# Clearing six experts' unused rows after the routing instead of before it

## The chip, the cores and the metric

One core of a Trainium2 chip runs the whole network in one launch. Its engines work side by side, each on its own list of instructions in order: TensorE (PE; PEld is its weight load), VectorE (DVE), ScalarE (ACT), GpSimd (POOL) and SyncE (SP). SP computes nothing here; it issues nearly all transfers, which 16 DMA engines carry out, and it takes its list in order too: an issue that waits holds up all behind it. The metric is the device time of one execution in microseconds (us); lower is better.

## The reference, cut to what matters

```python
for t in range(S):                                   # attention, 32 heads, 768 steps
    y[:, :, t] = einsum(r_t, state)
    Sa = einsum(state, a_t)
    state = state * w_t - Sa b_t + v_t k_t
...
expert_idx = argmax(x @ w_gate)                      # 3072 tokens, 8 experts
for i in range(N):                                   # each expert's rows, in order of arrival
    if counts[e] < capacity:
        disp[e, counts[e]] = x[i]; counts[e] += 1
h = maximum(einsum(disp, w1), 0); y = einsum(h, w2)  # all rows of disp, unused ones are zero
out[i] = gate_w[i] * y[expert_idx[i], pos[i]]
...
g = elu(x @ w_in); return g @ w_out                  # feed-forward, d_ff 2048
```

`disp` starts as zeros: rows that no token takes are zero. The capacity is 768 rows an expert.

## The kernel before

The kernel has three stages: the attention, the eight experts, and the feed-forward layer on tokens sorted by expert.

**The attention** cuts the sequence into 24 units of 64 steps (two halves of the batch, 12 chunks). Its order is written out by hand: the string `ORDER` and then `slot(k)` name steps by a letter and a unit, and each name issues the next part of that step. Every engine executes its own part of that list in order. `e`, `v`, `d` load inputs (L230, L234, L238); `p`, `a` scale them (VectorE L243 to L255, ScalarE L264); `c` makes score matrices and stores them to memory (L277, L291); `l` loads them back in the layout of the solve (L330); `i` is the triangular solve on GpSimd (L351, L353) for a group of two or four units; `o` stores its result (L359), and `t` loads that (L374 to L385); `f`, `g` complete the inverse; `r`, `u`, `w`, `s`, `q`, `y`, `x` make the unit's output and the next state; `b`, `j` find each token's expert and row. `D` scatters the unit's tokens to their rows of `disp` in memory with an indirect transfer of GpSimd.

`disp` has eight regions of `ES` = 3,584 rows of 329 numbers, one an expert; an expert's tokens start at row `ES * e + SL`, with `SL` = 448. `Z` followed by an expert's number is `zero_d` (L619): a store of zeros over the expert's 448 rows from that start, from a small cleared piece of memory on the chip, in 752-byte pieces. All eight `Z` stand ahead of the first scatter `D`: `Z7` early, `Z2`, `Z4`, `Z3`, `Z0`, `Z6`, `Z5`, `Z1` among the preparation of units 8 to 12.

**The experts** run as blocks b = 0 to 7 of `run`. A block loads its 448 rows (L1084) one block ahead, at step 0 of the block before. It has 8 steps f. In each, TensorE makes the hidden layer (L968) and, three steps later, the second product (L1031 to L1041); ScalarE and VectorE make the two parts of the hidden layer (L1097, L1098). At f = 0 and 4 SP fetches half an expert's weights (L801, L803), and ScalarE and GpSimd split earlier ones into two parts (L775, L780). After its last product a block stores its rows to `xt`, sorted by expert, at columns whose start stands in a register (L1206 to L1208).

`more(b, f)`, called at the end of each step, does two other things. `counts()` (`ct`) makes the experts' counts from the routing, their running sums (`cs`, `bi`, L1340, L1341), the number of rounds, and loads registers of SP with the sums at b = 1, f = 2 (L1355). `rest` converts the feed-forward layer's weights from 64-bit numbers: loads (L822, L825), eight operations of VectorE for each piece (L858 to L870), stores (L830, L834); it begins at b = 0, f = 5. Its first call there issues the loads of the first three pieces, and its operations stand in VectorE's list before that step's later work.

**The feed-forward stage** loads sorted columns from `xt`, multiplies, and scatters the result.

Of the kernel before, what the change touches and what calls it, by code (L numbers as in the profile page):

```python
# [8 lines left out]
F32 = mybir.dt.float32  # L9
F32R = mybir.dt.float32r  # L10
I32 = mybir.dt.int32
U32 = mybir.dt.uint32
AF = mybir.ActivationFunctionType
ALU = mybir.AluOpType
# [8 lines left out]
SL = 448  # L23
ES = 8 * SL
RW = 329
# [7 lines left out]
KR = 5  # L33
ORDER = """
se1 sa0 se0 se0 v1 sc0 e0.0 sv se1 e0.1 sd p0 sw p0 e1.0 sw a0 p0 v0 p1 sa1 sx a0 p1 lw sz st1 e2.0 c0.0 a1
p2 p2 a1 c0.0 e1.1 sr1 Z7 c0.1 p1 e3.0 c0.1 k0.0 k0.1 c0.1 c1.0 e2.1 a2 a2 c1.0 p3 c1.1 k1.1 k1.0 c1.1 k1.0 e4.0 d1 k1.1
c1.1 e3.1 m0.0 l0 m0.1 k0.1 p2 p3 a3 l1 a3 p4 p4 p3 m1.1 c2.1 e5.0 k2.1 c2.0 c2.1 m1.0 r0 c2.0 k2.0 k0.0 a4 m2.1 a4 p5
st0 k2.0 k3.1 sc1 c3.0 c2.1 c3.1 ss1 k3.0 e4.1 m2.0 p4 r0 r1 c4.0 i0 e6.0 k3.0 n0 k3.1 m3.0 k4.1 p5 n1 o0 c3.1 p6
c3.0 e5.1 a5 a5 c3.1 m3.1 k2.1 r1 e7.0 l2 p5 k4.1 c4.1 k4.0 m4.1 e6.1 c4.0 c5.1 k5.1 l3 p6 k5.0 c5.0 c4.1 p7 c4.1 p6 a6
m5.0 a6 v2 v3 p7 c5.0 t1 m4.0 t0 c6.1 m6.1 c5.1 k4.0 f1 k6.1 c5.1 k6.0 k6.1 m5.1 sr0 a7 i1 c6.0 f1 f0 a7 o1 e7.1 e8.0 f1 f0  # L40
k5.0 p7 c6.1 f0 f1 f1 p8 c6.0 d0 e9.0 f0 k5.1 c7.1 f0 f1 f1 c6.1 c7.0 f0 f0 e8.1 c7.1 g1 c7.0 g0 p8 m7.0 a8 ss0 p8 m7.1
g0 k7.1 l5 l4 g1 k7.0 k7.1 g0 k8.0 g0 c7.1 l6 p9 e9.1 g1 a8 u0 m6.0 p9 k6.0 k8.1 u0 g1 l7 c8.0 k7.0 m8.0 c8.1 n2 t2 e10
w0 a9 p9 f2 n3 k8.1 a9 q0.0 w0 q0.1 q0.1 w0 i2 u1 u1 f2 q0.0 c8.0 f2 p10 k9.1 c9.1 f2 c8.1 c9.0 m8.1 k8.0 Z2 c8.1 f2 w0
Z4 p10 t3 f2 s0 k9.1 p10 c9.1 c9.0 w1 w1 k9.0 y0 f2 i2 k9.0 g2 s0 w1 e11 s0 c9.1 f3 k10.1 Z3 r2 a10 w1 a10 f3 k10.1 m9.0
f3 y0 m9.1 k10.0 p11 Z0 r2 c10.0 q1.0 q1.0 c10.1 x0 f3 p11 h2 q1.1 s1 f3 g2 a11 k10.0 m10.1 i2 f3 c10.0 g2 q1.1 c10.1 h2
e12 v4 p11 f3 s1 c10.1 x0 y1 y1 d2 g3 p12 a11 s1 k11.1 c11.0 x1 g3 r3 Z6 c11.0 g2 g3 p12 k11.1 h3 x1 m11.0 a12 Z5 p12 x0 r3
u2 a12 c11.1 c12.0 u2 g3 w2 d3 c11.1 w2 k11.0 w2 x1 k12.1 h3 q2.0 q2.1 Z1 b0 w2 c11.1 c12.1 u3 c12.1 m10.0 m11.1 s2 j0
o2 u3 w3 k11.0 q2.1 q3.1 c12.0 e13 z2 q2.0 s2 w3 y2 s2 l11 j0 l10 y2 t4 m12.0 m12.1 r4 v5 l9 g4 d4 w3 k12.1 r4 p13 D0
h4 x2 l8 g4 c12.1 k12.0 D1 h4 t5 q3.0 p13 w3 g4 g4 g4 s3 u4 x2 a13 l12 s3 z3 q3.0 u4 w4 w4 a13 q3.1 p13 i3 w4 g5 h5 y3
d5 x2 w4 y3 s3 s4 i3 k12.0 e14 t6 s4 s4 h5 v6  # L50
# [635 lines left out]
def consts(p):  # L686

    c = {}
    c["ident"] = p.tile([128, 128], F32, name="ident")
    c["mask"] = p.tile([128, 64], F32, name="mask")  # L690
    for nm in ("ones", "tri"):
        c[nm] = p.tile([128, 128], BF, name=nm)
    c["desc"] = p.tile([128, 8], F32, name="desc")
    c["ebase"] = p.tile([128, 8], F32, name="ebase")
    c["lg"] = p.tile([128, 24, 9], F32, name="LG")
    c["oh"] = p.tile([128, 2, 8, 12], BF, name="OH")
    c["slot"] = p.tile([128, 24], I32, name="SLOT")
    c["acc"] = p.tile([128, 2, 8], BF, name="ACC")
    c["cap"] = p.tile([128, 2], I32, name="CAP")
    return c  # L700
# [42 lines left out]
class Ring:  # L743
# [8 lines left out]
    def next(s, split):  # L752
        k = s.turn[split]
        s.turn[split] += 1
        return s.tile((1, 4, 6, 8)[k % 4], F32R) if split else s.tile((0, 3)[k % 2], F32)
# [39 lines left out]
def expert(nc, ring, w1, w2, e, paired=True):  # L795
    def load(g, R):
        q = R.rearrange("p (f x) -> p f x", x=704)
        c = slice(512 * g, 512 * g + 512)
        for k, (o, r, m) in enumerate(((0, 0, 128), (0, 128, 128), (0, 256, 64), (64, 256, 64))):
            k = min(k, 2)  # L800
            nc.sync.dma_start(out=q[o:o + m, :, 128 * k:128 * k + 128],  # L801
                              in_=w1[e, r:r + m, c].rearrange("p (f x) -> p f x", x=128))
        nc.sync.dma_start(out=q[:, :, 384:704], in_=w2[e, c, :].rearrange("(f p) d -> p f d", p=128))  # L803
    return Weights(nc, ring, load, 8, paired)
# [73 lines left out]
def ahead(W):  # L878

    W.fetch(0)  # L880
    yield
    yield from W.split(0)
    W.fetch(1)


def ffn(tc, nc, cst, disp, xt, w1, w2, w32, out, ring, W0, cv):
# [3 lines left out]
    ap = ctx.enter_context(tc.tile_pool(name="fa", bufs=2))  # L890
# [289 lines left out]
            B.finish([p[1:] for p in lag])  # L1180


    dv = disp.rearrange("(e r i p) d -> e r p i d", e=8, i=4, p=112)

    W2 = Weights(nc, ring, lambda g, R: nc.sync.dma_start(out=R, in_=w32[g]), 16)

# [2 lines left out]
    def experts(r, dyn=False, more=None):  # L1189
# [43 lines left out]
        def extra(b, f):  # L1233
            if b >= 8:
                next(final, None)
                return
            if b == 0 and f > 1:
                next(first, None)
            i, ph = divmod(8 * b + f, 4)

            late = {(14, 0): 16, (14, 2): 17, (15, 2): 18}.get((i, ph)) if i > 13 else i + 2 if ph == 0 else None
            if late:
                gen[0] = split(late)
                fetch(late + 1)
            go(gen[0], 1 if i < 14 else 2)
            if more:
                more(b, f)
# [76 lines left out]
    over = {}  # L1324

    def counts():

        cw, cf = cst["cap"], ap.tile([128, 4], F32, name="cf", bufs=1)
        nc.vector.tensor_copy(cf[:, 0:2], cw)
        nc.vector.tensor_scalar(cf[:, 2:3], cf[:, 0:1], 0.0, 4294967296.0, op0=ALU.is_lt, op1=ALU.mult)  # L1330
        nc.vector.scalar_tensor_tensor(out=cf[:, 3:4], in0=cf[:, 1:2], scalar=4294967296.0, in1=cf[:, 2:3], op0=ALU.mult, op1=ALU.add)
        nc.vector.tensor_tensor(cf[:, 3:4], cf[:, 3:4], cf[:, 0:1], op=ALU.add)
        over["cap"] = cf[:, 3:4]
        p = ps.tile([128, 512], F32, tag="ph", name="pc")
        nc.tensor.matmul(p[:, 0:8], cst["ones"], cst["acc"][:, 0], start=True, stop=True)
        yield
        cnt = over["cnt"] = ap.tile([128, 8], F32, name="cnt", bufs=1)
        nc.vector.tensor_copy(cnt, p[:, 0:8])
        cs, bi = ap.tile([128, 8], F32, name="cs", bufs=1), ap.tile([128, 8], I32, name="bi", bufs=1)
        nc.vector.tensor_tensor_scan(out=cs, data0=over["one"], data1=cnt, initial=0.0, op0=ALU.mult, op1=ALU.add)  # L1340
        nc.vector.tensor_copy(bi, cs)  # L1341
        yield
        rn = ap.tile([128, 4], F32, name="rn", bufs=1)
        ri = ap.tile([128, 1], I32, name="ri", bufs=1)
        rg = ap.tile([128, 8], F32, name="rg", bufs=1)
        nc.vector.tensor_reduce(rn[:, 0:1], cnt, axis=AX.X, op=ALU.max)
        nc.vector.tensor_scalar(rn[:, 1:2], rn[:, 0:1], float(SL // 8), None, op0=ALU.add)
        nc.vector.tensor_scalar(rn[:, 2:3], over["cap"], float(SL), None, op0=ALU.min)
        nc.vector.tensor_tensor(rn[:, 2:3], rn[:, 0:1], rn[:, 2:3], op=ALU.is_gt)
        yield  # L1350
        nc.vector.tensor_scalar(rg, cst["ebase"], 1.0 / 8, rn[:, 1:2], op0=ALU.mult, op1=ALU.is_lt)
        nc.vector.tensor_reduce(rn[:, 3:4], rg, axis=AX.X, op=ALU.add)
        nc.vector.tensor_scalar(ri, rn[:, 3:4], rn[:, 2:3], 1.0, op0=ALU.mult, op1=ALU.add)
        yield
        _, over["base"] = nc.values_load_multi_w_load_instructions(bi[0:1, 0:7], (mybir.EngineType.SP,), min_val=0, max_val=NTOK)  # L1355
        yield
        over["n"] = nc.values_load(ri[0:1, 0:1], min_val=1, max_val=8)
# [47 lines left out]
    rest = cv.pieces(scratch, 28)  # L1405

    def more(b, f):
        if b == 0 and 0 < f < 5 or b == 1 and f in (2, 7):
            next(ct, None)
        if b or f > 4:  # L1410
            for _ in range(1 + f % 2):
                next(rest, None)
    one = over["one"] = ap.tile([128, 8], F32, name="one", bufs=1)
    nc.gpsimd.memset(one, 1.0)
    start = over["start"] = ap.tile([128, 6], F32, name="begin", bufs=1)
# [4 lines left out]
    cst["turn"] = ap.tile([128, 1], F32, name="turn", bufs=1)  # L1420
    nc.gpsimd.memset(cst["turn"], 0.0)
    ct = counts()
    experts(0, more=more)
    for _ in rest:
        pass
# [26 lines left out]
def network(tc, nc, e_in, v_tok, d_in, wg, cap, w1, w2, w_in, w_out, out):  # L1452
    with tc.tile_pool(name="cst", bufs=1) as p, tc.tile_pool(name="dsp", bufs=1, space=DRAM) as dp, tc.manual_schedule():
        cst = consts(p)
        disp = dp.tile([8 * ES, RW], F32, name="disp")
        xt = dp.tile([D + 1, XC], F32, name="xt")
        ring = Ring(p)
        w32 = dp.tile([4, 128, 2816], F32, name="w32")
        W0, cv = expert(nc, ring, w1, w2, 0), Convert(nc, w_in, w_out, w32)
        attention(tc, nc, e_in, v_tok, d_in, wg, disp, xt, cst, ring, ahead(W0), W0, cv, cap)  # L1460
        ffn(tc, nc, cst, disp, xt, w1, w2, w32, out, ring, W0, cv)
# [26 lines left out]
```

## Time and profile before

| | us |
|---|---|
| median of 3 runs | 1,066.04 (1,063.58 to 1,072.04) |
| the profiled execution | 1,064.33 |
| its span, first to last instruction | 1,062.6 |
| around the span | 1.7 |
| TensorE busy in the span | 965.8 (91%) |
| VectorE | 727.8 (68%) |
| GpSimd | 606.5 (57%) |
| ScalarE | 516.9 (49%) |
| mean granted TensorE clock, of 1 | 0.941 |

Times in the rows below count from the start of the span. A row of an engine in order of time gives its start, its length, the engine, the line, the operation, what it writes and reads, how many are merged (x), and in brackets how long the engine stood idle just before it and who released it. The share of busy time is an average over stages with different limits, so the stages are read one by one.

### The profile page before, as it was taken

What the parts mean: (1) busy time and instruction counts of PE and PEld (TensorE: products, weight loads), DVE (VectorE), ACT (ScalarE), POOL (GpSimd) and SP (SyncE); (2) the same over time, 40 slices, a digit from 0 to 9 for tenths busy, and PEclk for the clock granted to TensorE, in tenths of its full rate; (3) what the DMA queues carried; (4) which work ended last, traced back from release to release, by engine and by line L of the source; (5) the groups of instructions that cost most, each with busy time, mean ns of one, the idle gap of its engine ahead of it and who ended that gap; (6) DMA issues with size and microseconds to landing.
All of it is one profiled execution on the core that took longest, in us unless ns stands there. A gap on an engine that the chain in (4) does not pass through costs nothing.

```text
span 1062.6 us, 25351 instructions
## 1 busy us (share of the span) xinstructions
PE 965.8 (91%) x9995; PEld 871.9 (82%) x9995; DVE 727.8 (68%) x1287; ACT 516.9 (49%) x1011; POOL 606.5 (57%) x926
## 2 busy tenths in 40 slices
PE   5869978899899999888999999989999999999993
PEld 4758877798788889677889888869989989989983
DVE  8856756788674677549798963656766767776751
ACT  4646544556463334244535545454555455554551
POOL 4757839899898813456677876733323333323332
PEclk9866988899899889999999999989999999999997
DMA  6768675667654864576877765400101010100000
GB/s 165 163 179 197 168 137 105 151 131 141 139 110 103 192 164 103 155 203 168 230 218 209 221 193 188 161 23 3 48 1 32 19 26 25 26 25 1 26 1 28
DMA packets 180984, 121.67 MB, mean 115 GB/s; under 512 B 105792, under 2 KB 166872, under 8 KB 179224
## 3 DMA queue, kind: packets, MB, share of 16 engines
q1 hardware_dynamic: 176788, 102.89, 39.6%
q0 software_dynamic: 3168, 11.14, 3.0%
q10 hardware_dynamic: 900, 5.93, 2.2%
q8 instruction: 81, 1.33, 0.6%
q14 instruction: 47, 0.39, 0.1%
HBM read 86.87 MB, written 33.05 MB: 113 GB/s over the span
## 4 chain that ended last, share of the span: by engine, by line
PE 28%; issue 10%; POOL 6%; DVE 6%; DMA 4%; ACT 2%; SPq 1%; POOLq 0%; DVEq 0%; ACTq 0%
PE ph L968 14%; PE po L992 4%; PE po L994 4%; PE po L993 4%; POOL ring L780 3%; POOL L L1112 2%; DMA ring<-in_w_dram 2%; DVE L L1098 1%; ACT ring L775 1%; SPq L801 1%; DMA S<-in_w_in_dram 1%; DMA w<-E 1%; POOL out_dram L1282 1%; DVE E L859 1%; DVE M L867 1%
## 5 line engine op out<-in xcount | busy, mean ns | idle before, releaser
L780 POOL TENSOR_TENSOR ring<-ring,ring 128x64 fp32r<-128x64 f32 (+2 forms) x320 | 195.7, 647 | 90.0 <-ACT ring L775 87.7
L1112 POOL TENSOR_TENSOR L<-E,H 128x512 fp32r<-128x512 f32 x66 | 87.6, 1327 | 185.8 <-ACT H L1111 148.2
L968 PE MATMUL ph<-XH,ring 128*128 128x512 f32 (+1 forms) x640 | 172.9, 392 | 4.4 <-DVE L L1098 3.9
L968 PEld LDWEIGHTS ph<-XH,ring 128*128 128x128 f32 x640 | 117.4, 193 | 19.6 <-DVE L L1098 4.5
L1105 ACT ACTIVATE E<-N 128x512 f32<-128x512 f32 x96 | 60.7, 633 | 143.7 <-DVE N L1104 88.0
L992 PE MATMUL po<-ring,H 128*128 128x320 f32 x384 | 119.6, 311 | 5.5 <-ACT Y L1044 5.3
L353 POOL TENSOR_TENSOR X<-X,ring 128x60 f32<-128x60 f32 (+19 forms) x170 | 114.9, 676 | 13.3
L994 PE MATMUL po<-ring,L 128*128 128x320 f32 x384 | 119.6, 311 | 1.5 <-POOL L L1112 1.5
L993 PE MATMUL po<-ring,H 128*128 128x320 f32 x384 | 119.4, 311 | 0.0
L1104 DVE TENSOR_SCALAR N<-ph 128x512 f32<-128x512 f32 x96 | 65.9, 686 | 47.4 <-PE ph L968 47.0
L968 PE MATMUL ph<-XL,ring 128*128 128x512 f32 (+1 forms) x320 | 97.6, 386 | 0.0
L968 PE MATMUL ph<-XS,ring 128*128 128x512 f32 (+1 forms) x320 | 97.5, 386 | 0.0
L351 POOL TENSOR_TENSOR ring<-X,ring 128x60 f32<-128x60 f32 (+19 forms) x108 | 74.2, 687 | 39.0 <-DMA ring<-dab 18.2
L992 PEld LDWEIGHTS po<-ring,H 128*128 128x128 f32 x384 | 72.6, 189 | 10.5 <-ACT Y L1044 5.7
L993 PEld LDWEIGHTS po<-ring,H 128*128 128x128 f32 x384 | 72.7, 189 | 4.1
L994 PEld LDWEIGHTS po<-ring,L 128*128 128x128 f32 x384 | 72.9, 190 | 2.0 <-POOL L L1112 2.0
L1109 DVE SCALAR_TENSOR_TENSOR M<-E,M 128x512 f32<-128x512 f32 x96 | 70.7, 736 | 5.5 <-ACT M L1106 5.5
L775 ACT CAST ring<-ring 128x704 fp32r<-128x704 f32 x80 | 61.4, 779 | 21.3 <-issue 8.2
L1110 DVE SCALAR_TENSOR_TENSOR E<-ph,M 128x512 f32<-128x512 f32 x96 | 66.4, 691 | 7.8
L968 PEld LDWEIGHTS ph<-XL,ring 128*128 128x128 f32 x320 | 61.1, 191 | 10.8
L968 PEld LDWEIGHTS ph<-XS,ring 128*128 128x128 f32 x320 | 60.8, 190 | 10.8
L1111 ACT CAST H<-E 128x512 fp32r<-128x512 f32 x96 | 59.2, 617 | 15.1 <-DVE E L1110 12.0
(238 smaller groups left out, 2164.2 us busy)
## 6 DMA issues: line engine op xcount, KB each, us to landing
ring<-in_w_dram SPq DMA_DIRECT2D x16, 640.0 KB
ring<-in_w_dram SPq DMA_DIRECT2D x32, 256.0 KB
RVU<-in_d_in_dram SPq DMA_DIRECT2D x48, 160.0 KB
dab<-AB SPq DMA_DIRECT2D x24, 256.0 KB
ring<-in_e_in_dram ACTq DMA_DIRECT2D x18, 321.6 KB
ring<-w SPq DMA_DIRECT2D x4, 1408.0 KB
disp<-ring SPq DMA_DIRECT2D x8, 575.8 KB
ring<-in_w_dram SPq DMA_DIRECT2D x32, 128.0 KB
```

The source lines that it names most:

```text
L351: nc.gpsimd.tensor_tensor(tv, X[:, 0:n, s:s + 1].to_broadcast([128, n, m]), N[:, s:s + 1, s + 1:e].to_broadcast([128, n, m]), op=ALU.mult)
L353: nc.gpsimd.tensor_tensor(X[:, 0:n, s + 1:e], X[:, 0:n, s + 1:e], tv, op=ALU.subtract)
L775: s.nc.scalar.copy(B[:, 0:704], r)
L780: s.nc.gpsimd.tensor_tensor(B[:, to], r[:, q], B[:, q].bitcast(F32), op=ALU.subtract)
L968: nc.tensor.matmul(p, l, r[:, 0:s.T], start=i == 0, stop=i == len(seq) - 1)
L992: nc.tensor.matmul(o, H[:, c], hb, start=f == 0, stop=False)
L993: nc.tensor.matmul(o, H[:, c], lb, start=False, stop=False)
L994: nc.tensor.matmul(o, L[:, c], hb, start=False, stop=f == s.W.nf - 1)
L1104: nc.vector.tensor_scalar(N, p, 0.0, None, op0=ALU.min)
L1109: nc.vector.scalar_tensor_tensor(out=M, in0=E, scalar=1.0, in1=M, op0=ALU.add, op1=ALU.mult)
L1110: nc.vector.scalar_tensor_tensor(out=E, in0=p, scalar=0.0, in1=M, op0=ALU.max, op1=ALU.add)
L1112: eng.tensor_tensor(L, E, H.bitcast(F32), op=ALU.subtract)
```

## The change

Six of the eight `Z` leave the order of the attention; `Z0` stands where `Z7` stood and `Z1` where `Z2` stood. For the experts 2 to 7 a store of the same size, 448 rows, is issued by SP from `more`: expert 2's at b = 0, f = 5, those of experts 3 to 7 at b = 1 to 5, f = 3. It begins at the row behind the expert's last token, that is at `ebase` + count, which stands in a register, and so can run past the 448 rows that are used here (`disp` gets 448 rows more at its end). Its source is a new piece `zero`, which GpSimd clears at the start of the experts' stage. `counts()` adds those starts to the row of sums (`cs`, `bi` become 16 wide) and gets a part more, at b = 0, f = 3, which loads six registers of SP; its later parts move by one step at b = 0. The transfers of `disp` at a register's row are ordered with the loads of `disp` by waits, as all transfers of that tensor are.

```diff
-p2 p2 a1 c0.0 e1.1 sr1 Z7 c0.1 p1 e3.0 ...
+p2 p2 a1 c0.0 e1.1 sr1 Z0 c0.1 p1 e3.0 ...
...
-... k9.1 c9.1 f2 c8.1 c9.0 m8.1 k8.0 Z2 c8.1 f2 w0
-Z4 p10 t3 ... f3 k10.1 Z3 r2 a10 w1 a10 f3 k10.1 m9.0
-f3 y0 m9.1 k10.0 p11 Z0 r2 c10.0 ...
-e12 v4 p11 ... x1 g3 r3 Z6 c11.0 g2 g3 p12 k11.1 h3 x1 m11.0 a12 Z5 p12 x0 r3
-u2 a12 c11.1 ... h3 q2.0 q2.1 Z1 b0 w2 ...
+... k9.1 c9.1 f2 c8.1 c9.0 m8.1 k8.0 Z1 c8.1 f2 w0
+p10 t3 ... f3 k10.1 r2 a10 w1 a10 f3 k10.1 m9.0
...
-    dv = disp.rearrange("(e r i p) d -> e r p i d", e=8, i=4, p=112)
+    dv = disp[0:8 * ES].rearrange("(e r i p) d -> e r p i d", e=8, i=4, p=112)
...
-        cs, bi = ap.tile([128, 8], F32, name="cs", bufs=1), ap.tile([128, 8], I32, name="bi", bufs=1)
-        nc.vector.tensor_tensor_scan(out=cs, data0=over["one"], data1=cnt, initial=0.0, op0=ALU.mult, op1=ALU.add)
+        cs, bi = ap.tile([128, 16], F32, name="cs", bufs=1), ap.tile([128, 16], I32, name="bi", bufs=1)
+        nc.vector.tensor_tensor(cs[:, 8:16], cst["ebase"], cnt, op=ALU.add)
+        nc.vector.tensor_tensor_scan(out=cs[:, 0:8], data0=over["one"], data1=cnt, initial=0.0, op0=ALU.mult, op1=ALU.add)
         nc.vector.tensor_copy(bi, cs)
+        yield
+        _, v = nc.values_load_multi_w_load_instructions(bi[0:1, 10:16], (mybir.EngineType.SP,), min_val=0, max_val=8 * ES)
+        over["free"] = dict(zip(range(2, 8), v))
         yield
...
     def more(b, f):
-        if b == 0 and 0 < f < 5 or b == 1 and f in (2, 7):
+        if b == 0 and 0 < f < 6 or b == 1 and f in (2, 7):
             next(ct, None)
+        if b < 6 and f == (5, 3)[b > 0]:
+            r = bass.ds(over["free"][b + 2], SL)
+            nc.sync.dma_start(out=disp[r, :].rearrange("(p i) d -> p (i d)", p=112).rearrange("p (x d) -> p x d", d=188),
+                              in_=zero.unsqueeze(1).to_broadcast([112, 7, 188]))
         if b or f > 4:
             for _ in range(1 + f % 2):
                 next(rest, None)
+    zero = ap.tile([112, 188], F32, name="zero", bufs=1)
+    nc.gpsimd.memset(zero, 0.0)
...
-        disp = dp.tile([8 * ES, RW], F32, name="disp")
+        disp = dp.tile([8 * ES + SL, RW], F32, name="disp")
```

## Rows read from the trace of the kernel before

**Rows 1.** The clearing stores by line, and SP in order of time.

```profile
L619 SPq DMA_DIRECT2D disp<-ring x8: 621/689/2450, 12.2 to 121.9; - x8
...
87.73 0.65 SPq L619 DMA_DIRECT2D disp<-ring  x1
```

**Rows 2.** Stretches: length, busy time (instructions) by engine, clock, DMA share, GB/s.

```profile
83.00:131.00 48.00, 44.62 (x850) 41.55 (x851) 35.66 (x57) 28.57 (x64) 43.11 (x62) 0.84 0.77 185
152.00:375.00 223.00, 203.43 (x3832) 186.22 (x3832) 160.26 (x306) 112.00 (x249) 194.21 (x286) 0.92 0.63 137
443.80:485.50 41.70, 35.44 (x176) 30.51 (x176) 19.11 (x45) 20.16 (x38) 25.94 (x55) 0.96 0.63 172
...
477.40:500.40 23.00, 18.60 (x82) 16.13 (x83) 21.32 (x37) 8.89 (x17) 14.78 (x20) 0.93 0.61 170
```

**Rows 3.** GpSimd in order of time around one solve.

```profile
83.08 0.23 POOL L351 TENSOR_TENSOR ring<-X,LM 128x31 f32<-128x31 f32 x1 [11.37 <-DMA LM<-dab]
...
103.95 1.58 POOL L351 TENSOR_TENSOR ring<-X,LM 128x255 f32<-128x255 f32 x1
...
108.71 0.64 POOL L351 TENSOR_TENSOR ring<-X,LM 128x255 f32<-128x255 f32 x1
...
130.70 0.27 POOL L353 TENSOR_TENSOR X<-X,ring 128x31 f32<-128x31 f32 x1
...
138.34 0.97 POOL L342 MEMSET X<- 128x1024 f32 x1
...
152.10 0.37 POOL L351 TENSOR_TENSOR ring<-X,ring 128x31 f32<-128x31 f32 x1 [12.58 <-DMA TT<-dx]
```

**Rows 4.** SP in order of time, behind the end of the solve.

```profile
131.00 0.37 SPq L359 DMA_DIRECT2D dx<-X  x1
...
135.65 3.56 SPq L379 DMA_DIRECT2D TA<-dx  x1
...
147.02 1.02 SPq L330 DMA_DIRECT2D ring<-dab  x2
```

**Rows 5.** VectorE in order of time: two waits for transfers.

```profile
92.23 1.24 DVE L243 TENSOR_TENSOR_SCAN ring<-ring,DR 104x520 f32<-104x520 f32 x1 [3.04 <-DMA ring<-in_e_in_dram]
...
144.53 0.70 DVE L426 STREAM_TRANSPOSE AB<-TA 32x512 f32<-32x512 f32 x1 [6.20 <-DMA TA<-dx]
```

**Rows 6.** VectorE, then TensorE, in order of time, first expert.

```profile
459.48 0.24 DVE L1341 CAST bi<-cs 128x8 int32<-128x8 f32 x1
...
477.44 0.43 DVE L858 TENSOR_SCALAR N<-S 128x512 int32<-128x512 int32 x1 [7.41 <-DMA S<-in_w_in_dram]
...
479.19 1.08 PE L968 MATMUL ph<-XH,ring 128*128 128x448 f32 x4 [3.44 <-DVE L L1098]
```

**Rows 7.** SP in order of time, first expert.

```profile
455.89 0.60 SPq L803 DMA_DIRECT2D ring<-in_w_dram  x1
466.00 2.23 SPq L801 DMA_DIRECT2D ring<-in_w_dram  x4
...
468.92 2.54 SPq L822 DMA_DIRECT2D S<-in_w_in_dram  x4
```

**Rows 8.** Stretches of 2 us among the clearing stores.

```profile
118.00:120.00 2.00, 2.00 (x31) 1.91 (x30) 1.90 (x4) 1.25 (x4) 1.92 (x2) 1.00 1.02 277
...
124.00:126.00 2.00, 2.00 (x19) 2.00 (x20) 1.83 (x8) 1.96 (x5) 1.76 (x4) 1.00 1.08 251
```

**Rows 9.** Stretches of 4 us among the experts.

```profile
512.00:516.00 4.00, 4.00 (x21) 3.65 (x21) 2.76 (x5) 3.10 (x6) 4.00 (x8) 1.00 0.02 6
...
600.00:604.00 4.00, 4.00 (x21) 3.67 (x20) 3.19 (x5) 3.98 (x7) 3.37 (x6) 1.00 0.09 30
```

**Rows 10.** The register load of seven values on SP, by operation.

```profile
L1355 SPq FUSED_REGOPS  x7: 147/147/192, 498.0 to 499.9; - x7
...
L1355 SPq TENSOR_LOAD <-bi x1: 1153/1153/1153, 496.7 to 496.7; - x1
```

**Rows 11.** GpSimd in order of time, first expert.

```profile
454.62 4.25 POOL L780 TENSOR_TENSOR ring<-ring,ring 128x64 fp32r<-128x64 f32 x8 [1.63 <-ACT ring L775]
```

More of the change, by code (lines that the diff above doesn't have):

```diff
@@ L35 @@
 se1 sa0 se0 se0 v1 sc0 e0.0 sv se1 e0.1 sd p0 sw p0 e1.0 sw a0 p0 v0 p1 sa1 sx a0 p1 lw sz st1 e2.0 c0.0 a1
-p2 p2 a1 c0.0 e1.1 sr1 Z7 c0.1 p1 e3.0 c0.1 k0.0 k0.1 c0.1 c1.0 e2.1 a2 a2 c1.0 p3 c1.1 k1.1 k1.0 c1.1 k1.0 e4.0 d1 k1.1
+p2 p2 a1 c0.0 e1.1 sr1 Z0 c0.1 p1 e3.0 c0.1 k0.0 k0.1 c0.1 c1.0 e2.1 a2 a2 c1.0 p3 c1.1 k1.1 k1.0 c1.1 k1.0 e4.0 d1 k1.1
 c1.1 e3.1 m0.0 l0 m0.1 k0.1 p2 p3 a3 l1 a3 p4 p4 p3 m1.1 c2.1 e5.0 k2.1 c2.0 c2.1 m1.0 r0 c2.0 k2.0 k0.0 a4 m2.1 a4 p5
@@ L42 @@
 g0 k7.1 l5 l4 g1 k7.0 k7.1 g0 k8.0 g0 c7.1 l6 p9 e9.1 g1 a8 u0 m6.0 p9 k6.0 k8.1 u0 g1 l7 c8.0 k7.0 m8.0 c8.1 n2 t2 e10
[L43 to L47, printed above, removed]
+w0 a9 p9 f2 n3 k8.1 a9 q0.0 w0 q0.1 q0.1 w0 i2 u1 u1 f2 q0.0 c8.0 f2 p10 k9.1 c9.1 f2 c8.1 c9.0 m8.1 k8.0 Z1 c8.1 f2 w0
+p10 t3 f2 s0 k9.1 p10 c9.1 c9.0 w1 w1 k9.0 y0 f2 i2 k9.0 g2 s0 w1 e11 s0 c9.1 f3 k10.1 r2 a10 w1 a10 f3 k10.1 m9.0
+f3 y0 m9.1 k10.0 p11 r2 c10.0 q1.0 q1.0 c10.1 x0 f3 p11 h2 q1.1 s1 f3 g2 a11 k10.0 m10.1 i2 f3 c10.0 g2 q1.1 c10.1 h2
+e12 v4 p11 f3 s1 c10.1 x0 y1 y1 d2 g3 p12 a11 s1 k11.1 c11.0 x1 g3 r3 c11.0 g2 g3 p12 k11.1 h3 x1 m11.0 a12 p12 x0 r3
+u2 a12 c11.1 c12.0 u2 g3 w2 d3 c11.1 w2 k11.0 w2 x1 k12.1 h3 q2.0 q2.1 b0 w2 c11.1 c12.1 u3 c12.1 m10.0 m11.1 s2 j0
 o2 u3 w3 k11.0 q2.1 q3.1 c12.0 e13 z2 q2.0 s2 w3 y2 s2 l11 j0 l10 y2 t4 m12.0 m12.1 r4 v5 l9 g4 d4 w3 k12.1 r4 p13 D0
```

## The prediction

> **What bounds the kernel now.** I read the span cut into stages first, then the order of time on single engines where the eight stores stand and where six of them go.
>
> The stores lie between 12.23 and 121.90 us, the last seven of them from 87.73 on [rows 1]. In that stretch, 83 to 131 us, GpSimd is busy 43.1 of 48.0 us [rows 2]: it runs one triangular solve without a break, from 83.08, when the last table that the solve reads has landed, to 130.97 (130.70 + 0.27) [rows 3]. The other engines prepare later units meanwhile. What they run into is the end of that solve: SP stores its result at 131.00 and can issue the load of it at 135.65, behind the landing of the store; the table for the last unit of the next solve is issued at 147.02, by the order of SP's queue [rows 4]. VectorE waits 6.20 us for the loaded result, to 144.53 [rows 5], TensorE then for VectorE, and the next solve starts at 152.10 after 12.58 us of waiting [rows 3]. From 152 to 375 us GpSimd is busy 194 of 223 us [rows 2] with four more solves. So between 83 and 152 us the attention is paced by this chain: solve, store, loads, next solve. The reader is to see that none of its links is a clearing store.
>
> The experts begin at 443.8 us. The first one's stage, to 485.5, has TensorE at work for 35.4 of 41.7 us [rows 2]. Its largest loss is at 475.75: TensorE waits 3.44 us, to 479.19, for VectorE's L1098. VectorE had itself waited 7.41 us, to 477.44, for the first piece that the weight converter loads [rows 6]. That piece was issued at 468.92, right behind a fetch of expert weights at 466.00 [rows 7]; its landing sets the pace there.
>
> **The change part by part.** *Six stores leave the attention.* One is 448 x 329 x 4 = 589,568 bytes; its issue takes SP 0.69 us in the median [rows 1]. SP's queue and the transfers are relieved, but both wait for the solve's end anyhow: SP stands still for it until 131.00. Cover: the solve of 47.9 us. I put the gain at 0. Upper bound: if VectorE and TensorE were the chain, six transfers at the price below, 13 us. A loss is possible too: GpSimd's L351 takes 1.58 us at 103.95 and 0.64 at 108.71 for the same 255 columns [rows 3]; 13 of the solve's 62 operations are stretched so, by 10.7 us together. VectorE work that comes earlier could add some. I bound it at 3 more, 3 x 0.94 = 2.8 us. The two stores that stay are expert 0's at 12 us, in the place of expert 7's, and expert 1's in the place of expert 2's at 87.73: no price, since they are of the same size.
>
> *What a store's bytes cost where DMA is full.* From 118 to 120 us, with clearing stores in flight, 277 GB/s moved, from 124 to 126, behind them, 251 [rows 8]. 589,568 bytes take 2.1 us at the one and 2.35 at the other; I take 2.2. The Trainium skill, page "DMA: Bandwidth & Descriptors", section "Specifications", gives about 358 GB/s of HBM for a core. By it one store is an estimated 1.65 us and the sum below 1,066.0; the rows here, with these 752-byte pieces, decide for 2.2.
>
> *The first moved store* stands in the first expert's sixth step (b = 0, f = 5), in SP's program ahead of the converter's first loads, so between 466.00 + 2.9 and the issue that was at 468.92 [rows 7]. It waits for nothing that is late: the register is loaded by then (below), and the load of expert rows ahead of it left at the block's start, five steps before. Whatever lies behind it on SP's queue is the converter's first piece, and that is the landing on which VectorE stands in order, with L1098 and so TensorE behind it [rows 6]. DMA is full there. So the piece lands 2.2 us later, VectorE waits 9.6 instead of 7.4, TensorE 5.6 instead of 3.4: **+2.2 us**. From there to 500.4 us VectorE is busy 21.3 of 23.0 us [rows 2], so little of it can be won back. Bounds: 0, if the store's share fits beside the loads; 2.35 plus one issue of 0.69, 3.0, if all adds up.
>
> *The five others* stand at b = 1 to 5, f = 3, just after the result stores of the expert before and ahead of the second weight fetch. Each expert has a stretch with DMA almost idle before its successor begins: 512 to 516 us with 2% busy, 600 to 604 with 9% [rows 9]. These are 3.6 to 4 us long; 2.2 us more of transfers fits in. The expert's rows that they clear are loaded some 17 us later, at the next block's start. I put them at 0 each; bound above 2.2 each, 11 in all, where a landing that VectorE or the weight split stands on comes later.
>
> *Registers.* The new load of six values on SP (b = 0, f = 3) is priced by the one of seven at L1355: 1.15 us from 496.7 for the load, then arithmetic, the last of it begun at 499.9 [rows 10]: 3.3 us, and some 3 for six values. SP stands idle from 456.49 to 466.00 before the weight fetch [rows 7], and the counts are converted by 459.72 [rows 6], so it ends near 463: 0. Without that cover the fetch and all behind it would be late by up to 3 us. The later steps of the counts (b = 0, f = 4 and 5) move by one step; nobody reads them before b = 1.
>
> *Small work.* VectorE gets one addition of 128 x 8 (0.24 us by the conversion of 128 x 8 beside it [rows 6]), GpSimd one clearing of 112 x 188 (well under 0.97 us, which it takes for 128 x 1,024 [rows 3]). GpSimd waits 1.63 us for ScalarE at 454.62 [rows 11], which covers the second; the first falls into VectorE's work before the 7.41 us of waiting. Both 0. Bound: 1.2 together.
>
> Sum: 0 + 2.2 + 0 + 0 + 0 = +2.2 us on the profiled execution's 1,064.33: 1,066.5. The median of the runs shown is 1.7 us above that execution, which would give 1,068.2. I put **1,067.4**, between.
>
> **The rivals.** (1) *Every store costs its transfer among the experts.* For it: at the first one DMA is full, and a store at a register's address begins at any row, which no row here prices; against it: the idle stretches [rows 9]. Six times 2.2 is 13.2: 1,077.5 on own time, 1,079 on the median. It decides once the idle stretch before each expert is used up, that is if a store takes over 3.6 us, or if VectorE stands on landings in every expert. 14%, slower by over 1%.
>
> (2) *The preparation, not the solve, paces 83 to 131 us, and the relief counts.* For it: VectorE waits 3.04 us, to 92.23, for a load that stands among the stores [rows 5]. If the six transfers came off, 13.2 us, less 2.2 in the experts, the time would be 1,053.3 (1,055 on the median). Against it: VectorE, and TensorE behind it, then wait 6.2 us for the solve, so anything they gain makes that wait longer. It decides only where the solve ends sooner than its helpers are done, and that isn't so. 7%, faster by over 1%.
>
> (3) *The first store is hidden as well*: its writes go beside the converter's reads, 0 us: 1,064.3 to 1,066. 17%.
>
> (4) *GpSimd's solve gets longer* by VectorE work that comes earlier: +2.8 + 2.2, 1,069.3 to 1,071. The Trainium skill, page "SBUF — State Buffer", section "SBUF: two separate sides", says that VectorE and GpSimd share one pair of ports, held for a whole instruction; the doubled L351 [rows 3] agrees with it. 8%. That the change doesn't do what it says, a store that clears rows it needn't or none, would not show in the time.
>
> **How the numbers follow.** Forecast 54%, (1) 14, (2) 7, (3) 17, (4) 8. Both signs of a large effect are unlikely, so the range leaves out the extremes of (1) and (2): 1,058 to 1,076. The likeliest case alone, with its bounds 0 and 3.0 and the 1.7 between execution and median, spans 1,064.3 to 1,069.0. A measurement of this kernel tells about 1%, 10.7 us, from no change (its three runs lie 8.5 apart): faster 7%, slower 13%, within 80%.
>
> **What would show it.** In the profile after: the solve between 83 and 131 us unmoved within 3 us and the first VectorE wait behind it still there and longer; the experts beginning at 441 to 447 us (443.8 before); TensorE's wait near 479 us grown from 3.4 to about 5.6; the next five stores without a new wait of TensorE over 1 us. I'm wrong if the experts begin at 435 or sooner (rival 2), if expert periods after the first grow by 2 us each (rival 1), or if SP's weight fetch at 466 is late by the register load.

## The result and the profile after

| | before | after |
|---|---|---|
| median of 20 runs, us | 1,065.92 (1,059.64 to 1,072.95) | 1,071.19 (1,065.38 to 1,079.02) |
| ratio, with its 95% interval | | 1.0056 [1.0037, 1.0075] |
| the profiled execution, us | 1,064.33 | 1,073.67 |
| its span | 1,062.6 | 1,072.0 |

The kernel became slower by 5.3 us. That is half of the 10.7 us that the prediction called a change, and more than the 1.5 us (1,067.4 less 1,065.92) that it forecast. The ratios here and below are estimates from the fast runs alone (a few runs fall into a slower state), not quotients of the two medians.

The page of the kernel after, its first lines: span, then busy time, share and instructions by engine.

```profile
span 1072.0 us, 25378 instructions
PE 967.6 (90%) x9995; PEld 870.2 (81%) x9995; DVE 728.9 (68%) x1288; ACT 516.9 (48%) x1011; POOL 607.2 (57%) x927
```

TensorE is busy 1.8 us longer than before (967.6 against 965.8). The other 7.6 of the 9.4 us that the span grew are time in which it stands, so the question is which wait grew.

The stores of `disp` in the kernel after, by line (the form of [rows 1]).

```profile
L1416 SPq DMA_DIRECT2D disp<-zero x6: 655/682/709, 473.6 to 624.4; - x6
...
L619 SPq DMA_DIRECT2D disp<-ring x2: 647/680/714, 12.2 to 87.6; - x2
```

Six stores have moved and two stay, as the diff says. Their issues cost SP what they cost before.

GpSimd around the same solve, after (the form of [rows 3]).

```profile
83.18 0.23 POOL L351 TENSOR_TENSOR ring<-X,LM 128x31 f32<-128x31 f32 x1 [11.25 <-DMA TA<-dab]
...
130.72 0.27 POOL L353 TENSOR_TENSOR X<-X,ring 128x31 f32<-128x31 f32 x1
...
152.32 0.33 POOL L351 TENSOR_TENSOR ring<-X,ring 128x31 f32<-128x31 f32 x1 [11.68 <-DMA dab<-AB]
```

Stretches of the kernel after (the form of [rows 2]).

```profile
83.00:131.00 48.00, 43.14 (x840) 40.16 (x839) 34.31 (x55) 29.07 (x65) 43.03 (x62) 0.85 0.46 111
...
152.00:375.00 223.00, 203.55 (x3749) 185.68 (x3746) 159.50 (x303) 110.54 (x246) 195.04 (x286) 0.92 0.62 133
```

From 83 to 131 us the DMA share fell from 0.77 to 0.46 and the rate from 185 to 111 GB/s. Yet the solve starts 0.1 us later than before and the next one 0.2 later. So the relief reached the queues, and the pace did not notice it.

The first expert in the kernel after: SP, then VectorE, then TensorE, in order of time (the forms of [rows 7] and [rows 6]).

```profile
448.03 1.76 SPq L1084 DMA_DIRECT2D X<-disp  x4
...
470.48 2.25 SPq L801 DMA_DIRECT2D ring<-in_w_dram  x4
472.76 0.60 SPq L803 DMA_DIRECT2D ring<-in_w_dram  x1
473.59 0.71 SPq L1416 DMA_DIRECT2D disp<-zero  x1
474.35 3.71 SPq L822 DMA_DIRECT2D S<-in_w_in_dram  x4
...
485.95 0.43 DVE L858 TENSOR_SCALAR N<-S 128x512 int32<-128x512 int32 x1 [10.85 <-DMA S<-in_w_in_dram]
...
487.69 1.86 PE L968 MATMUL ph<-XH,ring 128*128 128x448 f32 x4 [7.47 <-DVE L L1098]
...
494.04 0.57 SPq L1084 DMA_DIRECT2D X<-disp  x1
```

The store stands between the weight fetch and the converter's loads. VectorE's wait for the first piece grew from 7.41 to 10.85 us, TensorE's for VectorE from 3.44 to 7.47. The stage, from the first load of expert rows to the one at block 1's start, took 46.01 us (494.04 - 448.03); before it took 41.72, from 443.81 to 485.53.

This divides the 9.4 us of the span: the experts begin 4.22 us later, their first stage is 4.29 us longer, and the rest 0.89. Which of these belongs to the change is for the experiments to say; the solve above, which stands where it stood, speaks against the first.

### The profile page after: what moved, and what is told of

Read it like the earlier page. It is cut to its first block, busy times and chain, and to the rows that moved or that the text cites. A ratio compares the mean times of both kernels' runs of the same rounds, so it can differ in the third digit from the quotient of the medians.

```text
span 1072.0 us, 25378 instructions
## 1 busy us (share of the span) xinstructions
PE 967.6 (90%) x9995; PEld 870.2 (81%) x9995; DVE 728.9 (68%) x1288; ACT 516.9 (48%) x1011; POOL 607.2 (57%) x927
## 4 chain that ended last, share of the span: by engine, by line
PE 28%; issue 9%; DMA 6%; DVE 5%; POOL 5%; ACT 2%; SPq 1%; POOLq 0%; DVEq 0%; ACTq 0%
PE ph L968 14%; PE po L992 4%; PE po L994 4%; PE po L993 4%; POOL L L1112 2%; POOL ring L780 2%; DMA S<-in_w_in_dram 2%; DMA ring<-in_w_dram 1%; DVE L L1098 1%; ACT ring L775 1%; DMA w<-E 1%; POOL out_dram L1282 1%; DMA xt<-Y 1%; DVE N L858 1%; DVE N L869 1%
## 5 line engine op out<-in xcount | busy, mean ns | idle before, releaser
L968 PE MATMUL ph<-XH,ring 128*128 128x512 f32 (+1 forms) x640 | 172.3, 391 | 10.0 <-DVE L L1098 9.4
L968 PEld LDWEIGHTS ph<-XH,ring 128*128 128x128 f32 x640 | 116.5, 191 | 25.8 <-DVE L L1098 10.9
L353 POOL TENSOR_TENSOR X<-X,ring 128x60 f32<-128x60 f32 (+19 forms) x170 | 123.3, 725 | 13.3
L968 PE MATMUL ph<-XS,ring 128*128 128x512 f32 (+1 forms) x320 | 97.5, 386 | 0.2 <-DVE XS L953 0.2
L968 PE MATMUL ph<-XL,ring 128*128 128x512 f32 (+1 forms) x320 | 97.6, 386 | 0.0
L968 PEld LDWEIGHTS ph<-XS,ring 128*128 128x128 f32 x320 | 60.7, 190 | 11.2 <-DVE XS L953 0.5
L968 PEld LDWEIGHTS ph<-XL,ring 128*128 128x128 f32 x320 | 61.0, 191 | 10.9
```

What stands on the lines that cost most here:

```text
L353: nc.gpsimd.tensor_tensor(X[:, 0:n, s + 1:e], X[:, 0:n, s + 1:e], tv, op=ALU.subtract)
L968: nc.tensor.matmul(p, l, r[:, 0:s.T], start=i == 0, stop=i == len(seq) - 1)
```

## The experiments

Each run is read in the same three places: the experts' start (the first L1084), the first stage (to the load at block 1's start), and the rest (to the end of the span). "Issue to piece" is the time from the first issue, of the store or of the converter's loads, to VectorE's L858 on the first piece. All come from the profiled executions.

| kernel | stores ahead of the piece | start | stage | issue to piece | VectorE's wait | TensorE's wait | rest |
|---|---|---|---|---|---|---|---|
| before | none | 443.81 | 41.72 | 8.52 | 7.41 | 3.44 | 577.07 |
| e1_behind | none | 441.45 | 40.89 | 7.61 | 5.89 | 2.51 | 577.96 |
| e2_relief | none | 444.06 | 40.28 | 6.50 | 5.40 | 1.43 | 579.56 |
| e4_five | none | 442.81 | 41.13 | 7.07 | 5.37 | 2.02 | 580.96 |
| e5_one | one, even start, fixed | 445.21 | 43.64 | 9.88 | 8.73 | 4.76 | 577.65 |
| e12_one | the same | 448.51 | 44.07 | 10.80 | 9.69 | 5.72 | 578.52 |
| e11_reg | one, even start, register | 445.14 | 44.24 | 10.45 | 8.91 | 5.53 | 577.62 |
| e10_odd | one, shifted start, fixed | 442.82 | 45.67 | 12.12 | 11.01 | 7.04 | 579.71 |
| after | one, shifted start, register | 448.03 | 46.01 | 12.36 | 10.85 | 7.47 | 577.96 |
| e13_after | the same | 442.22 | 46.26 | 12.52 | 11.03 | 7.65 | 579.32 |
| e3_first | the same | 448.13 | 46.18 | 12.04 | 10.50 | 7.13 | 580.89 |
| e6_two | two, even start, fixed | 446.30 | 48.63 | 13.99 | 12.53 | 8.56 | 578.07 |
| e7_before_early | none, piece loaded early | 446.10 | 36.32 | | 0 | 0 | 578.38 |
| e8_after_early | one, piece loaded early | 444.83 | 36.04 | | 0 | 0 | 579.53 |

"Even" stands for a store that begins at a multiple of 448 rows, "shifted" for one that begins 414 rows further. A row is 329 x 4 = 1,316 bytes. 448 rows are a multiple of 64 bytes; 414 rows are 544,824 bytes, 56 past such a multiple. Expert 2 has 414 tokens, so the store of the changed kernel begins as the shifted one does.

**Only where the store stands.** In e1_behind each late store follows the step's converter calls.

```diff
     def more(b, f):
         ...
-        if b < 6 and f == (5, 3)[b > 0]:
-            ... store of expert b + 2's rows
         if b or f > 4:
             for _ in range(1 + f % 2):
                 next(rest, None)
+        if b < 6 and f == (5, 3)[b > 0]:
+            ... store of expert b + 2's rows
```

> The changed kernel, with each late store issued behind the converter's calls of the same step, so that at b = 0, f = 5 it stands behind the first three pieces instead of ahead of them. Queue theory (the first store's bytes delay the piece on which VectorE stands, the rest is small): VectorE's wait for the first piece falls from 10.9 us back to about 7.4, TensorE's from 7.5 to 3.4, and the time from +5 us over the kernel before to +1. Rival A (the attention got longer, as the profile shows experts starting 4.2 us later): still +4 to +5 with the experts starting near 448. Rival B (the five other stores or the register load carry the loss): still +4 to +5, lost behind 494 us.

Measured: 1,070.05 us, ratio 1.0029 [0.9998, 1.0059]. SP, then VectorE, of e1_behind in order of time:

```profile
466.63 2.43 SPq L822 DMA_DIRECT2D S<-in_w_in_dram  x4
469.29 0.74 SPq L1419 DMA_DIRECT2D disp<-zero  x1
...
474.24 0.43 DVE L858 TENSOR_SCALAR N<-S 128x512 int32<-128x512 int32 x1 [5.89 <-DMA S<-in_w_in_dram]
```

The store now leaves behind the loads, and the wait is no longer than before. All six stores are still late, and the stage is 40.89 us instead of 46. So the stage's 4 to 5 us come from what the store stands ahead of, not from its being there. The median is still 2.9 us above that of before, with an interval that touches 1; the profiled execution shows nothing of it in the stage, and I leave it open.

**The relief alone.** In e2_relief nothing is late. Where each expert's 448 rows were cleared, six of the stores clear their last 112 rows or, for expert 1, 224: 784 rows instead of 2,688.

```diff
     zero_d(e):
+        n = {7: 448, 2: 448, 1: 224}.get(e, 112)
+        c = n * 47 // 112
-        ... disp[e * ES + SL:e * ES + 2 * SL, :] in pieces of 188 numbers
+        ... disp[e * ES + 2 * SL - n:e * ES + 2 * SL, :] in pieces of c numbers
```

> The kernel before, with nothing late; the six stores among the preparation stay at their places but clear only the last 112 rows (expert 1: 224), 784 rows instead of 2,688, so 71% of their bytes are gone (rows that a token fills in these inputs are no longer cleared first). Theory: the solve paces 83 to 152 us, so relief is worth nothing: 0 us, within 2. Rival A (the relief makes the attention longer): +3 to +4. The rival of the prediction (the preparation paces): -8 to -9.

Measured: 1,069.47 us, ratio 1.0030 [0.9997, 1.0064]; the experts begin at 444.06, against 443.81 before. A relief that counted would have given about 0.992, the 8 to 9 us that were expected of it. Taking most of those bytes away brought nothing. As a test of the relief this run is weaker than it looks: each store keeps its 784 pieces, only smaller ones (188 bytes instead of 752, 376 for expert 1), and from 83 to 131 us the DMA share fell just from 0.77 to 0.72, the rate from 185 to 133 GB/s. The kernel after, where the share fell to 0.46, is the stronger test, and its solve stands where it stood.

**The first store, and the five others.** In e3_first only expert 2's store is late, in e4_five only those of experts 3 to 7; the rest stand in the attention.

```diff
 # e3_first (Z3 to Z7 are back in ORDER)
-        if b < 6 and f == (5, 3)[b > 0]:
+        if b == 0 and f == 5:
 # e4_five (Z2 is back in ORDER)
-        if b < 6 and f == (5, 3)[b > 0]:
+        if 0 < b < 6 and f == 3:
```

> The changed kernel with expert 2's store alone late (b = 0, f = 5); the experts 3 to 7 are cleared in the attention, seven stores there. Queue theory: nearly the whole loss stays, +4 us; VectorE's wait for the first piece near 10.9, TensorE's near 7.5. Rival B: +1 or less. Rival A (relief of six): +1.

> The changed kernel with expert 2's store back in the attention (three stores there) and the five others late (b = 1 to 5, f = 3), the register load included. Queue theory: TensorE's wait at the first piece back at 3.4 us, +1 us over the kernel before. Rival A (relief): +4. Rival B: +4.

Measured: e3_first 1,073.66 us, 1.0049 [1.0015, 1.0082]; e4_five 1,067.05 us, 1.0009 [0.9976, 1.0042]. One store alone carries the loss, and five carry none that can be measured. These two intervals overlap; what parts the two kernels clearly is the stage: 46.18 and 41.13 us.

**The store's own price.** e5_one is the kernel before with one more store at b = 0, f = 5, at a fixed address with an even start; e6_two has two. No routing, register or other order is touched.

```diff
 # before
+        if b == 0 and f == 5:
+            for k in range(1):        # e6_two: range(2)
+                r = slice(2 * ES + (2 + k) * SL, 2 * ES + (3 + k) * SL)
+                nc.sync.dma_start(out=disp[r, :]..., in_=zero...)
```

> The kernel before with all its stores, and one more clearing store of the same size at b = 0, f = 5 ahead of the converter's loads, at a fixed address among rows that nothing reads; no register load, no relief. Queue theory (what costs is the transfer's place, not the register or the odd start row): VectorE's wait for the first piece grows from 7.4 to about 10.5 to 11 us, TensorE's from 3.4 to about 7, the first expert's stage (41.7 us before, 46.0 changed) to about 46, +4 to +5 in all. Rival (a store at a register's address, at any row, is slower than a plain one): VectorE's wait near 9.6, the stage near 43.9, +2.

> As the kernel with one more store, but with two of them there, to different rows. If a store costs its bytes at the full rate of 277 GB/s, the second adds 2.1 us to VectorE's wait; by what the first one cost, 3.1 to 3.4 us: a wait of about 14 us and a first stage of 49 to 50 us, +8.

Measured: e5_one 1,070.00 us, 1.0018 [0.9992, 1.0044]; e6_two 1,074.42 us, 1.0049 [1.0023, 1.0076]. SP, then VectorE, then TensorE, of e5_one in order of time:

```profile
470.90 0.65 SPq L1413 DMA_DIRECT2D disp<-zero  x1
471.60 3.51 SPq L822 DMA_DIRECT2D S<-in_w_in_dram  x4
...
480.78 0.43 DVE L858 TENSOR_SCALAR N<-S 128x512 int32<-128x512 int32 x1 [8.73 <-DMA S<-in_w_in_dram]
...
482.52 1.86 PE L968 MATMUL ph<-XH,ring 128*128 128x448 f32 x4 [4.76 <-DVE L L1098]
```

An even store lengthens the stage from 41.0 (mean of the four without) to 43.6, a second one by 5.0 more. So the store is real work on the path, but one even store gives only half of what the changed kernel shows. The stage of about 46 that I expected of e5_one was missed; 43.6 is what the rival said (43.9), whose cause, the register's address, was not yet tested. The second store of e6_two adds 3.8 us to VectorE's wait (12.53 less 8.73), more than either price expected of it, and the reason stays open: from 478.9 to 480.9 us that kernel moved 137 GB/s at a DMA share of 1.16. A difference between it and the changed kernel's store was still to be found: the register's address, or the row at which it begins.

**Register or row.** e10_odd is e5_one with the start moved by 414 rows and the address still fixed. e11_reg has all eight `Z` in the attention, the change's register load and a store at a register's address, whose value is a multiple of 448 rows. e12_one repeats e5_one, and e13_after the changed kernel, beside them.

```diff
 # e10_odd, against e5_one
-            r = slice(2 * ES + 2 * SL, 2 * ES + 3 * SL)
+            r = slice(2 * ES + 2 * SL + 414, 2 * ES + 2 * SL + 414 + SL)
 # e11_reg, against after (all Z back in ORDER)
-        nc.vector.tensor_tensor(cs[:, 8:16], cst["ebase"], cnt, op=ALU.add)
+        nc.vector.tensor_scalar(cs[:, 8:16], cst["ebase"], float(SL), None, op0=ALU.add)
-        if b < 6 and f == (5, 3)[b > 0]:
+        if b == 0 and f == 5:
```

> The kernel before with one more store at b = 0, f = 5, at a fixed address, but beginning 414 rows further, at the row where expert 2's late store begins within its 448 (its pieces then begin at odd multiples of 8 bytes, not of 16). No register load. Theory C (an odd start row makes the store's bytes slower): from the store's issue to the converter's first piece about 12.2 us as in the changed kernel, the first stage near 46. Theory D (the start row doesn't matter): 9.9 us and 43.6 as with the even row.

> All eight stores stay in the attention; one more at b = 0, f = 5 at a register's address, register load included, but the register holds an even start row among rows that nothing reads. Theory C (odd row): 9.9 us from the store's issue to the piece, first stage near 43.6. Theory E (the register's address or the register load costs): about 12.2 us and 46.

> The same kernel as the one with one more store at a fixed even row, once more, to see how far one execution's wait can be trusted: if its first stage of 43.6 us is typical, it comes out within 43 to 44.5 again; if single executions differ by more, anywhere from 42 to 46.

> The changed kernel once more beside the three others, for the same reason: VectorE's wait for the first piece was 10.9 us and the first stage 46.0; if these are typical, 10 to 11.5 and 45 to 47, and the time +5 us. The experts' start, 448.0 in its profile, would come out anywhere from 441 to 448 if the attention varies from one execution to the next, and near 448 again if the change lengthens it.

Measured, all against the same runs of before (median 1,068.14):

| kernel | start row, address | median, us | ratio |
|---|---|---|---|
| e12_one | even, fixed | 1,071.43 | 1.0038 [1.0013, 1.0063] |
| e11_reg | even, register | 1,070.76 | 1.0045 [1.0016, 1.0075] |
| e10_odd | shifted, fixed | 1,074.78 | 1.0075 [1.0046, 1.0105] |
| e13_after | shifted, register | 1,073.53 | 1.0072 [1.0040, 1.0104] |

SP, then VectorE, of e10_odd in order of time:

```profile
468.30 0.65 SPq L1412 DMA_DIRECT2D disp<-zero  x1
469.00 4.33 SPq L822 DMA_DIRECT2D S<-in_w_in_dram  x4
...
480.42 0.43 DVE L858 TENSOR_SCALAR N<-S 128x512 int32<-128x512 int32 x1 [11.01 <-DMA S<-in_w_in_dram]
```

SP, then VectorE, in e11_reg:

```profile
470.84 0.71 SPq L1416 DMA_DIRECT2D disp<-zero  x1
...
481.29 0.43 DVE L858 TENSOR_SCALAR N<-S 128x512 int32<-128x512 int32 x1 [8.91 <-DMA S<-in_w_in_dram]
```

Stretches of 2 us of e10_odd, from 3.7 us behind the store's issue on (columns as in [rows 8]; the last three are the clock, the DMA share and GB/s):

```profile
472.00:474.00 2.00, 2.00 (x12) 1.83 (x11) 0.00 (x0) 0.40 (x1) 0.00 (x0) 1.00 1.18 237
474.00:476.00 2.00, 1.13 (x6) 0.65 (x4) 0.00 (x0) 0.00 (x0) 0.00 (x0) 1.00 1.21 150
476.00:478.00 2.00, 0.00 (x0) 0.00 (x0) 0.00 (x0) 0.00 (x0) 0.00 (x0) 1.00 1.01 179
```

The same of e5_one, from 3.1 us behind the store's issue on:

```profile
474.00:476.00 2.00, 2.00 (x14) 1.87 (x13) 0.00 (x0) 0.53 (x1) 0.30 (x1) 1.00 1.06 335
476.00:478.00 2.00, 1.76 (x9) 1.22 (x7) 0.00 (x0) 0.00 (x0) 0.00 (x0) 1.00 1.20 234
478.00:480.00 2.00, 0.00 (x0) 0.00 (x0) 0.00 (x0) 0.00 (x0) 0.00 (x0) 1.00 0.97 316
```

In both the DMA engines are full, at a share of 0.97 or more. With the even start they move 295 GB/s in the mean of these three stretches, with the shifted one 189. Taken at one distance from the store's issue, 4 to 10 us behind it, it is 275 to 283 GB/s in the three executions with an even start and 185 to 222 in the four with a shifted one. The trace also holds each packet with its duration. In this place the store's 784 pieces took 51 to 52 ns each in the mean with an even start and 68 to 80 with a shifted one; over 16 engines that is 2.5 us and 3.3 to 3.9. So the store's packets take the engines longer. But the row alone doesn't do it: the shifted store of e1_behind, which stands behind the loads, took 46 ns a piece, and the two even stores of e6_two 67.

The address makes no difference that shows: an even start has a stage of 43.64 and 44.07 us with a fixed address and 44.24 with a register. The row does: a shifted start has 45.67 with a fixed address, 46.01, 46.26 and 46.18 with a register. The means are 41.0 without a store, 44.0 even, 46.0 shifted. From issue to piece it is 7.4, 10.4 and 12.3 us, so the same 589,568 bytes hold the piece up by 3.0 us or by 4.8 us. Both contain the 0.70 to 0.77 us by which the converter's loads leave SP behind the store's issue, so they are not the time of the bytes alone. The intervals of the medians overlap; it is the stages, three or four executions a kind with no overlap between kinds, that carry this. What it is in a shifted start that makes the packets slower in this place (the remainder of 56 bytes, or something else about those rows) was not separated: one shift only was run.

**Taking the wait away.** e7_before_early is the kernel before, and e8_after_early the kernel after, with the converter's first two loads issued two steps earlier, at b = 0, f = 3, into buffers that stand free. (Of the converter's two calls at f = 5 the first issues the loads of two pieces, the second those of the third; the first call is the one that moves.)

```diff
+        if b == 0 and f == 3:
+            next(rest, None)
         if b or f > 4:
-            for _ in range(1 + f % 2):
+            for _ in range(1 + (f % 2 and (b, f) != (0, 5))):
                 next(rest, None)
```

> The kernel before with the loads of the converter's first two pieces issued at b = 0, f = 3, ahead of the weight fetch of f = 4, instead of at f = 5. Queue theory: the piece has landed when VectorE comes to it, its wait of 7.4 us and TensorE's of 3.4 vanish; the first stage takes 37 to 39 us instead of 41.7, and the time falls by 3 to 5 us. Rival (the weights of the next half expert then come late and TensorE waits for them): no gain.

> The changed kernel with the same two loads at b = 0, f = 3. Queue theory: the late first store stands behind them, so nothing waits for its bytes: the first stage again 37 to 39 us instead of 46, the time 3 to 4 us under the kernel before and 8 under the changed one. Rival (the store's bytes delay the weight fetch or the third piece just as much): the first stage 3 us over that of the other kernel with early loads.

Measured: e7_before_early 1,062.23 us, 0.9937 [0.9909, 0.9965]; e8_after_early 1,062.46 us, 0.9946 [0.9918, 0.9973]. Both beat the kernel before by 6 us, which is more than was expected of e7_before_early (3 to 5) and of e8_after_early (3 to 4). Against the kernel after, which did not run beside them, their medians are 9 to 11 us lower. VectorE of e8_after_early and, ahead of it, SP, in order of time:

```profile
464.46 0.83 SPq L822 DMA_DIRECT2D S<-in_w_in_dram  x2
...
470.50 0.71 SPq L1416 DMA_DIRECT2D disp<-zero  x1
471.27 2.69 SPq L822 DMA_DIRECT2D S<-in_w_in_dram  x2
...
471.96 0.81 DVE L858 TENSOR_SCALAR N<-S 128x512 int32<-128x512 int32 x1
```

L858 has no bracket: VectorE didn't wait. The stage takes 36.3 and 36.0 us instead of 41.7 and 46.0, TensorE's wait at the piece is gone (it has none over 0.9 us in the stage), and the change, its late store shifted and all, costs 0.2 us in the medians. The landing of that piece was the whole of the price that can be measured, and the change's stores cost nothing once nothing stands on it.

## Why the prediction was right, and where its size was off

**The attention, 0: right in size.** The solve stands where it stood. The experts begin at 443.9 us in the mean of the six executions with the relief (after, e13_after, e1, e2, e4, e8; 441.45 to 448.03) and at 445.8 in that of the eight with seven or more whole stores there (442.82 to 448.51). The 1.9 us between the means are less than the scatter of either kind, so a small gain can't be excluded; one of 13 us is. The 4.2 us that the first pair loses here are scatter too: the changed code began at 448.03 and at 442.22. The prediction's mark, 441 to 447, was missed by one of these and hit by the other. One sign of it went another way: it expected VectorE's wait for the solve's result to stay and grow, but the bracket fell from 6.20 us [rows 5] to 3.18. VectorE in the kernel after, in order of time:

```profile
139.12 0.69 DVE L556 TENSOR_TENSOR XT<-y,GE 104x512 f32<-104x512 f32 x1 [2.83 <-remote]
...
144.18 0.70 DVE L426 STREAM_TRANSPOSE AB<-TA 32x512 f32<-32x512 f32 x1 [3.18 <-DMA TA<-dx]
```

The result reached it at 144.18 instead of 144.53, so the pace is the one named, but VectorE came to that wait later than before, not sooner. The relieved queues did not make the preparation run ahead in this execution.

**The first store, +2.2: right in place and mechanism, short in size.** This is the step that was mis-sized: it measured +5.0 us (stage 46.0 against 41.0), beyond the bound of 3.0 that the prediction gave it. Two things are in it. An even store holds the piece up by 3.0 us and lengthens the stage by 3.0. That is the prediction's bound for "if all adds up": its pieces take the DMA engines 2.5 us, a little over the 2.2 from the rates of [rows 8], and the loads behind it leave SP 0.70 us later, which the likeliest case put at nothing. How much of that issue lay on the path was not separated. The other 2.0 us come, in this place, from the row at which the store begins; in e10_odd the DMA engines moved 150 and 179 GB/s in two stretches of 2 us. The prediction had noticed that "a store at a register's address begins at any row, which no row here prices", and put it only into rival (1); a term that no row prices belonged into the bound of the first store as well. TensorE's wait grew by 4.0 us (7.47 less 3.44) instead of the 2.2 expected. The Trainium skill, page "DMA: Bandwidth & Descriptors", section "Specifications", gave an estimated 1.65 us by its 358 GB/s; the runs show 3.0 and 4.8, so here the measurement decides against it.

**The five others, 0: right.** The rest behind the first stage takes 579.2 us in the mean of the five executions with them late and 578.6 in that of the nine without, each from 577 to 581. TensorE in the kernel after, its longest wait from 494 to 660 us, in which the five stores lie:

```profile
563.75 0.47 PE L1032 MATMUL po<-H,ring 128*128 128x448 f32 x1 [2.00 <-DVE Y L1045]
```

Before, the same line waited 1.79 us at 554.37. The prediction's mark, no new wait over 1 us, holds. e4_five confirms it on the median. Rival (1), the same price at every store, falls.

**Registers, 0: right.** The register load in the kernel after, by operation (the form of [rows 10]):

```profile
L1344 SPq FUSED_REGOPS  x6: 147/147/187, 466.0 to 467.3; - x6
...
L1344 SPq TENSOR_LOAD <-bi x1: 1502/1502/1502, 464.4 to 464.4; - x1
```

It is over by 467.5, three us before the weight fetch at 470.48, so it stayed under its cover.

**The sum.** The first stage alone gives 5.0 us, against 5.3 (1,071.19 less 1,065.92) and 5.4 (1,073.53 less 1,068.14) in the medians; the ratios, 1.0056 and 1.0072, give 6.0 and 7.7 with wide intervals. The means of the rest, +0.6, and of the start, -1.9, lie within their scatter; with them the sum would be 3.7, so it does not close to better than some 2 us. The range of 1,058 to 1,076 holds the 1,071.19, but the likeliest case by itself reached only to 1,069.0: it is the width given for the rivals that took in the mis-sized term, and that is luck. The measured time lies next to rival (4)'s 1,069.3 to 1,071 by chance, since its cause did not come. Rivals (2), (3) and (4) each foresaw something that did not come: a large gain in the attention, a store that is hidden, a longer solve (47.81 us after, from 83.18 to 130.99, and 47.89 before).

## What to carry to other kernels

When a transfer is put ahead of a load that an engine stands on, price it at what the load loses, its issue included, from a run with that one transfer added at the very rows it will use, and not from the rate of a busy stretch alone. A piece that is waited for at the start of a stage is worth loading earlier: here two loads moved by two steps gave 6 us and made the moved stores free, where moving the stores behind the loads brought the stage back to 40.9 us but gave no gain over the kernel before. And where two profiled executions of the same code differ by 6 us, read a small change stage by stage over several runs of several edits, not from one pair.

## What the runs showed of the hardware that was not expected

- Between a weight fetch and the converter's loads, what a store costs depends on the row at which it begins: the same 589,568 bytes in 752-byte pieces held the next load up by 3.0 us at an even start and by 4.8 us when the store began 414 rows further (56 bytes past a multiple of 64), with the DMA engines full in both. It is not a property of the row alone: behind the loads the shifted store's pieces took 46 ns each, no longer than even ones, and those of two even stores in a row 67. Whether the address came from a register made no difference that shows.
- TensorE came out of the long wait at a lower clock. Stretches of the kernel after around it (columns as in [rows 2]):

```profile
478.00:482.00 4.00, 2.22 (x11) 1.64 (x9) 0.00 (x0) 0.00 (x0) 0.00 (x0) 1.00 1.15 181
482.00:486.00 4.00, 0.00 (x0) 0.00 (x0) 0.05 (x1) 0.00 (x0) 0.00 (x0) 0.66 0.96 244
486.00:490.00 4.00, 2.31 (x6) 2.11 (x7) 3.34 (x6) 1.63 (x3) 0.28 (x1) 0.50 0.29 72
```

After 7.47 us of waiting the granted clock was 0.50, the lower of its two levels (1.2 GHz), and L968 took 1.86 us for four matmuls instead of 1.08 [rows 6]. The length of this wait doesn't decide it by itself: before, TensorE came out of 3.44 us with a granted clock of 1.00 from 478 to 480 us and 1.08 us for the four, and in e1_behind out of 2.51 us with 0.50 from 476 to 478 and again 1.86:

```profile
475.98 1.86 PE L968 MATMUL ph<-XH,ring 128*128 128x448 f32 x4 [2.51 <-DVE L L1098]
```

In the first pair the longer wait makes 4.03 of the 4.29 us by which the stage grew. Behind the stage another wait went: before, TensorE stood 2.61 us at 493.46 for VectorE's L1050, and after it did not.

- The attention's length differs between executions of the same code by 6 us, from 442.22 to 448.03 for the changed kernel, more than the whole change.
